# Fused adaLN, attention and Mish MLP: Mish stages moved between ScalarE and VectorE, and fixed probability buffers

## The chip, the cores and the metric

The kernel runs on one core of a Trainium2 chip. The metric is the device time of one execution in microseconds (us). The core has five engines with instruction queues of their own: TensorE (PE in the profile, with PEld for its weight loads), VectorE (DVE), ScalarE (ACT), GpSimd (POOL) and SyncE (SP), which here issues the DMAs. Each engine works its queue in order; engines wait for each other by semaphores. Three runs of the kernel before took 1747.57, 1747.98 and 1752.33 us; the median is 1747.98.

## The reference

One transformer block over a sequence of 2048 positions of width 512, in fp32. Shifts, scales and gates come from a conditioning vector.

```
mod = silu(c) @ w_mod                       # sa, ca, ga, sb, cb, gb
h = layernorm(x) * (1 + ca) + sa
q, k, v = split(h @ wqkv)                   # 32 heads of 16
p = softmax(q k^T / 4);  o = p v
x = x + ga * (o @ wo)
h = layernorm(x) * (1 + cb) + sb
t = h @ w1 + b1                             # 512 to 1792
act = t * tanh(softplus(t))                 # Mish
x = x + gb * (act @ w2)                     # 1792 to 512
```

## The kernel before

**Attention.** Queries are taken in four blocks of 512, heads in eight groups of four: 32 pairs of block and group (n), each in 16 steps over the keys, so 512 steps t (T), with 20 (PRO) ahead of them that only compute maxima, and a few behind. In a step (function `step`), TensorE computes four score products for the current pair (line 507; ScalarE takes their exponentials at line 510), four products for the maxima of scores 20 steps ahead (line 470; VectorE reduces each at line 472), and at the end of the step the values' product of the step two back (`pv`, line 525; four matmuls that the trace shows as eight). The scores contract over half of the array's rows, so the score and maximum products use one half, and beside them, on the other half, run matmuls of other work.

**Other work.** Everything else of the layer is cut into units: projections to q, k and v, the output projection (`wo_unit`), the up products of the MLP (`up_unit`, one for each of 14 tiles f of 128 features) and the down products (`down_unit`). A unit has 12 or 15 matmuls over the full 128 rows; `step` issues them as matmuls on 64 rows (`mm_half`, line 132), first half of the unit on the lower rows and then on the upper rows: six beside each step for four steps (a unit of 12), or eight and seven (a unit of 15). All accumulate in one PSUM bank, `bk`. When the last matmul of a unit is issued, its `fin` issues what empties the bank: for an up unit the ScalarE instruction of line 701 (`s1`), for the output projection the VectorE addition of line 770. The bank must be empty before the next unit begins. Steps with no unit ready run the eight products on both halves.

**Ring of banks.** Scores, maxima and single products go through a ring of six PSUM banks (`ring`); a product takes the bank of the sixth product before it, and so waits for the exponential or reduction that read it.

**What sets the order.** The program is written out in the order in which the generator calls the engines; a scheduler does not reorder it. Functions are hung on half-steps: `at(h, f)`, where h = 2t is the start of step t and h = 2t + 1 its middle, after the first half of the products. `done["a", f]` is the half-step at which the activation of tile f counts as ready; a down unit is queued five half-steps after that of its last tile. `cur["after"]` holds the instruction for which the first unit matmul of the next step waits: the consumer of the product issued beside the previous step's last unit matmul, where `product()` returns one. Scores return their exponential, maxima return nothing.

**Mish.** Function `mish` computes for a tile, with e = exp of the capped input: hb = t (line 701), the clamp (704, Relu of 10 - t on ScalarE), ee = exp(10 - clamp) (707), ee = ee (ee + 2) (710, VectorE), hb = hb ee (711, POOL), rr = ln(ee + 2) (714), rr = exp(-rr) (717), then on POOL one Newton step for the reciprocal and the product (723 to 727), and the split of the result into a high and a low part, `a_h` (95) and `a_l` (98). The stages after `s1` stand at half-steps 1, 2, 3, 4 and 6 behind it. In the last query block, behind the loop, the function `tail` runs the same on ScalarE and VectorE.

**MLP blocks in the loop.** The output projection, layernorm and MLP of query blocks 0 to 2 are units in the loop (3 x 14 = 42 up units); the fourth block and the end of the third are in `tail`: output projection (895), layernorm (104 to 109), the down units still held back (126, 829, 830), then the fourth MLP.

**Probability buffers.** Each exponential writes a tile `pr` from a pool, three in rotation for heads 0 and 2 of a group, four for 1 and 3. Reusing one waits for the values' product that read it.

Of the kernel before, what the change touches and what calls it, by code (L numbers as in the profile page):

```python
# [18 lines left out]
def adaln_block(ctx: ExitStack, tc: tile.TileContext, x, wqkv, wo, w1, b1, w2, c, w_mod, out):  # L19
# [442 lines left out]
    def max_tile(n, j, s, qs, kb):  # L462

        if n not in mxs:
            mxs[n] = ap.tile([P, 2, 8, 4], F32, tag="mx", name="mx", bufs=2)

        def product():
            kt, qt = ka[(2 * n + j) % NR], qa[(2 * n + j) % NR]
            pm = ring()
            nc.tensor.matmul(pm, qt[64 * s:64 * s + 64, qs * P:(qs + 1) * P], kt[64 * s:64 * s + 64, kb * TB:(kb + 1) * TB],  # L470
                             start=True, stop=True)
            nc.vector.tensor_reduce(out=mxs[n][:, s, 4 * j + qs, kb:kb + 1], in_=pm, op=ALU.max, axis=AX.X)  # L472

        return product

# [22 lines left out]
                        mt[o:o + 8, :].bitcast(F32))  # L498
        at(2 * (16 * n + 16 - PRO) + 3, put)

    pts = {}

    def score(n, j, s, kc):
        def product():
            kt, qt = ka[(2 * n + j) % NR], qa[(2 * n + j) % NR]
            p_ = ring()
            nc.tensor.matmul(p_, kt[64 * s:64 * s + 64, kc * P:(kc + 1) * P], qt[64 * s:64 * s + 64, :],  # L507
                             start=True, stop=True)
            pr = ap.tile([P, TB], F32, tag=f"p{2 * j + s}", name="pr", bufs=3 + s)
            e = nc.scalar.activation(pr, p_, AF.Exp, scale=SCALE)  # L510
            pts[16 * n + kc, 2 * j + s] = pr
            return e
        return product
# [173 lines left out]
    def mish(f, acc, tail):  # L687

        mp = mst["p"]
        hb = mp.tile([P, TB], F32, tag="hb", name="hb", bufs=3)  # L690
        ee = mp.tile([P, TB], F32, tag="ee", name="ee", bufs=2)
        rr = mp.tile([P, TB], F32, tag="rr", name="rr", bufs=2)
        qq = mp.tile([P, TB], F32, tag="qq", name="qq", bufs=1)
        a_h = mp.tile([P, TB], F32R, tag="a_h", name="a_h", bufs=NA)
        a_l = mp.tile([P, TB], F32R, tag="a_l", name="a_l", bufs=NA)

        def s1(late=False):
            if late:
                nc.vector.tensor_scalar_add(hb, acc, b1c[:, f:f + 1])
            else:  # L700
                nc.scalar.activation(hb, acc, AF.Identity, bias=b1c[:, f:f + 1])

        def s2():
            nc.scalar.activation(ee, hb, AF.Relu, bias=hcap, scale=-1.0)

        def s2b():
            nc.scalar.activation(ee, ee, AF.Exp, bias=hcap, scale=-1.0)  # L707

        def s3():
            nc.vector.scalar_tensor_tensor(ee, ee, 2.0, ee, op0=ALU.add, op1=ALU.mult)  # L710
            (nc.vector if tail else nc.gpsimd).tensor_mul(hb, hb, ee)  # L711

        def s4():
            nc.scalar.activation(rr, ee, AF.Ln, bias=two)

        def s5():
            nc.scalar.activation(rr, rr, AF.Exp, scale=-1.0)  # L717
            if tail:
                nc.vector.scalar_tensor_tensor(qq, ee, 2.0, rr, op0=ALU.add, op1=ALU.mult)
                nc.vector.scalar_tensor_tensor(rr, qq, 2.0, rr, op0=ALU.subtract, op1=ALU.mult)  # L720
                nc.vector.scalar_tensor_tensor(hb, hb, -1.0, rr, op0=ALU.mult, op1=ALU.mult)
            else:
                nc.gpsimd.tensor_scalar(ee, ee, 1.0, 2.0, op0=ALU.mult, op1=ALU.add)
                nc.gpsimd.tensor_mul(qq, ee, rr)  # L724
# [3 lines left out]
            hi_copy("v" if tail and f > FT - 4 else "p", a_h, hb)  # L728
            lo_sub("v" if tail and f > FT - 4 else "p", a_l, hb, a_h)

        return (a_h, a_l), (s1, s2, s2b, s3, s4, s5)

    def idle(h):

        return h is not None and 2 * (T - PRO) + 2 < h <= 2 * T
# [4 lines left out]
    def block(qb, t0):  # L740
# [61 lines left out]
        def up_unit(f, tag):  # L802
            w = w1s.pop(f)
            acc = bank(tag)
            up_mms(acc, w, *hx)
            act[f], stages = mish(f, acc, False)

            def fin(h):
                stages[0](idle(h))
                for i, s in zip((1, 2, 3, 4, 6), stages[1:]):  # L810
                    at(h + i, s)
                done["a", f] = h + 6
                if f == FT - 1 and qb == NB - 2:
# [62 lines left out]
    def tail():  # L876

        oh, ol = o_hl[last]
        mp = mst["p"]
        y, xn = [], []  # L880
        for v in (y, xn):
            for i in range(4):
                v.append(ap.tile([P, D], F32, tag=f"p{i}", name="y", bufs=3 + i % 2))
        for i in range(4):
            r = 4 * last + i
            nc.sync.dma_start(y[i], x[r * P:(r + 1) * P, :])
# [140 lines left out]
    def step(t):  # L1027
        second = t % 2
        n, u = t // 16, t % 16 // 2
        tm = t + PRO  # L1030
        run_hooks(2 * t)
        if t < 0:

            for i in range(2):
                if tm < 16:
                    kb, jq = divmod(2 * tm + i, 8)
                else:
                    jq, kb = tm % 16 // 2, 2 * second + i
# [24 lines left out]
        if tm < T:  # L1063
            o = max(0, (8 - f) // 2)
            mo, alone = maxima(tm // 16, tm % 16 // 2, s, o)

            mine = [x for p in zip(mo, own) for x in p] + own[len(mo):]
        else:
            o = max(0, (4 - f) // 2)
            mine = own[o:] if second else own[:4 - o]  # L1070
            alone = others[4 - o:] if second else others[:o]

            m = len(mine)
            if f > m:
# [131 lines left out]
    for pp, h in ((2, -22), (3, -8)):  # L1206
        at(h, lambda pp=pp: load_pair(pp))
    def run_hooks(h):
        for f in hooks.pop(h, []):
            f()  # L1210

    for t in range(-PRO, T + 2):
        step(t)
# [34 lines left out]
```

## Time and profile before

| | |
|---|---|
| median of three runs | 1747.98 us |
| the profiled execution, span | 1752.7 us |
| TensorE busy | 1711.7 us |
| VectorE busy | 1464.5 us |
| ScalarE busy | 1341.6 us |
| GpSimd busy | 751.4 us |
| attention exponentials (line 510) | 2048, mean 604 ns |
| reductions of maxima (line 472) | 2048, mean 683 ns |

The profiled execution is one further execution with the hardware profiler on; times of trace rows are microseconds from its start. A row of the timeline reads: start, duration, engine, line, operation, output<-inputs, shapes, count of equal instructions in a row, and in brackets how long the engine stood idle before and what released it. A matmul's row shows its modelled end, so successive rows overlap. The granted TensorE clock was full (0.996 on the mean).

### The profile page before, as it was taken

How to read it: one execution, taken by the hardware profiler on the slowest of the kernel's cores; microseconds unless marked ns; L12 is line 12 of the kernel's file. 1: busy time of each engine (PE TensorE's matmuls, PEld its weight loads, DVE VectorE, ACT ScalarE, POOL GpSimd, SP SyncE). 2: the span in 40 equal slices, each digit the busy share in tenths (PEclk: the TensorE clock that was granted, in tenths of full speed). 3: DMA queues.
4: the chain of work that ended last, by engine and by line, in shares of the span. 5: the costliest groups of instructions: out<-in, count | busy, mean ns of one | idle time of the engine just before them, and what ended most of it. 6: DMA issues, size and time to landing. Idle time of an engine off the chain costs nothing.

```text
span 1752.7 us, 33365 instructions
## 1 busy us (share of the span) xinstructions
PE 1711.7 (98%) x12230; PEld 954.7 (54%) x12230; DVE 1464.5 (84%) x2464; ACT 1341.6 (77%) x2565; POOL 751.4 (43%) x740
## 2 busy tenths in 40 slices
PE   7999999999999999999999999999999999999999
PEld 5755665555435455555455455555455455554687
DVE  6888888887888998888989898888989899891477
ACT  6247777777777898797877898797877799897464
POOL 5145224656303275263312276173412267162852
PEclk9999999999999999999999999999999999999999
DMA  7676467777662342432435443442435434422451
GB/s 236 181 234 196 119 170 208 236 238 220 207 196 63 110 117 71 143 101 67 104 108 144 126 114 80 121 120 52 120 82 158 113 102 102 126 79 71 153 228 61
DMA packets 113996, 240.05 MB, mean 137 GB/s; under 512 B 24048, under 2 KB 49648, under 8 KB 107784
## 3 DMA queue, kind: packets, MB, share of 16 engines
q1 hardware_dynamic: 113832, 237.92, 47.5%
q8 instruction: 96, 1.57, 0.4%
q14 instruction: 68, 0.56, 0.1%
HBM read 179.95 MB, written 51.44 MB: 132 GB/s over the span
## 4 chain that ended last, share of the span: by engine, by line
PE 80%; DMA 6%; DVE 4%; ACT 3%; POOL 3%; issue 2%; SPq 2%; POOLq 0%; ACTq 0%; DVEq 0%
PE bk L525 26%; PE ring L470 20%; PE ring L507 18%; PE bk L132 11%; DVE mx L472 3%; ACT pr L510 2%; DMA qscr<-ql 2%; PE ring L126 2%; PE ring L963 1%; PE bk L126 1%; DMA kscr<-ql 1%; DMA wr<-in_A_wqkv 1%; DMA w2scr<-hl 1%; DMA vg<-vscr 0%; SPq L317 0%
## 5 line engine op out<-in xcount | busy, mean ns | idle before, releaser
L472 DVE TENSOR_REDUCE mx<-ring 128x1 f32<-128x512 f32 x2048 | 1273.9, 683 | 176.9 <-PE ring L470 145.1
L510 ACT ACTIVATE pr<-ring 128x512 f32<-128x512 f32 x2048 | 1080.7, 604 | 274.7 <-PE bk L132 148.2
L470 PE MATMUL ring<-ka,qa 64*128 64x512 f32 x2048 | 847.6, 431 | 1.1 <-DVE mx L472 0.2
L507 PE MATMUL ring<-qa,ka 64*128 64x512 f32 x2048 | 737.4, 401 | 11.8 <-ACT pr L510 10.5
L470 PEld LDWEIGHTS ring<-ka,qa 64*128 64x128 f32 x2048 | 364.8, 184 | 398.3 <-DVE mx L472 321.8
L525 PE MATMUL bk<-pr,vg 128*32 128x512 f32 x4096 | 547.0, 606 | 0.0
L507 PEld LDWEIGHTS ring<-qa,ka 64*128 64x128 f32 x2048 | 372.5, 185 | 119.9 <-ACT pr L510 64.3
L132 PE MATMUL bk<-h,w 64*128 64x512 f32 x996 | 275.9, 409 | 1.4 <-ACT pr L510 1.2
L132 PEld LDWEIGHTS bk<-h,w 64*128 64x128 f32 x996 | 171.1, 184 | 17.5 <-ACT pr L510 7.7
L132 PE MATMUL bk<-w,a_h 64*128 64x512 f32 x576 | 167.2, 414 | 0.3
L525 PEld LDWEIGHTS bk<-pr,vg 128*32 128x32 f32 x4096 | 80.7, 108 | 138.6 <-issue 133.4
L830 POOL TENSOR_TENSOR y<-yd,y 128x512 f32<-128x512 f32 x40 | 51.9, 1303 | 214.2 <-ACT yd L829 193.6
L711 POOL TENSOR_TENSOR hb<-hb,ee 128x512 f32<-128x512 f32 x42 | 53.9, 1284 | 178.2 <-DVE ee L710 178.2
L132 PEld LDWEIGHTS bk<-w,a_h 64*128 64x128 f32 x576 | 96.4, 184 | 12.0 <-ACT pr L510 6.7
L724 POOL TENSOR_TENSOR qq<-ee,rr 128x512 f32<-128x512 f32 x42 | 54.4, 1295 | 75.3 <-ACT rr L717 72.7
L132 PE MATMUL bk<-w,o_hl 64*128 64x512 f32 x288 | 80.6, 411 | 1.6 <-POOL o_hl L95 1.0
L132 PE MATMUL bk<-w,a_l 64*128 64x512 f32 x288 | 76.9, 390 | 0.0
L98 POOL TENSOR_TENSOR a_l<-hb,a_h 128x512 fp32r<-128x512 f32 x53 | 72.3, 1363 | 4.4
L132 PE MATMUL bk<-h_h,wl 64*128 64x512 f32 x168 | 57.2, 421 | 0.0
L710 DVE SCALAR_TENSOR_TENSOR ee<-ee 128x512 f32<-128x512 f32 x56 | 39.8, 711 | 19.3 <-ACT ee L707 19.3
L727 POOL TENSOR_TENSOR hb<-hb,rr 128x512 f32<-128x512 f32 x42 | 54.4, 1296 | 3.3
L132 PEld LDWEIGHTS bk<-w,a_l 64*128 64x128 f32 x288 | 53.0, 184 | 4.8
(186 smaller groups left out, 1735.8 us busy)
## 6 DMA issues: line engine op xcount, KB each, us to landing
ka<-kscr SPq DMA_DIRECT2D x124, 384.0 KB
w<-w2scr SPq DMA_DIRECT2D x56, 512.0 KB
w<-w1scr SPq DMA_DIRECT2D x46, 512.0 KB
vg<-vscr SPq DMA_DIRECT2D x32, 552.0 KB
qa<-qscr SPq DMA_DIRECT2D x124, 100.0 KB
kscr<-qh SPq DMA_DIRECT2D x16, 512.0 KB
qscr<-qh SPq DMA_DIRECT2D x32, 256.0 KB
hl<-in_B_w SPq DMA_DIRECT2D x28, 256.0 KB
```

What stands on the lines that cost most here:

```text
L98: (nc.gpsimd if eng == "p" else nc.vector).tensor_sub(lo, src, hi.bitcast(F32))
L126: nc.tensor.matmul(acc, l, r, start=start, stop=stop)
L132: i = nc.tensor.matmul(acc, l[64 * g:64 * g + 64], r[64 * g:64 * g + 64], start=start, stop=stop)
L470: nc.tensor.matmul(pm, qt[64 * s:64 * s + 64, qs * P:(qs + 1) * P], kt[64 * s:64 * s + 64, kb * TB:(kb + 1) * TB], start=True, stop=True)
L472: nc.vector.tensor_reduce(out=mxs[n][:, s, 4 * j + qs, kb:kb + 1], in_=pm, op=ALU.max, axis=AX.X)
L507: nc.tensor.matmul(p_, kt[64 * s:64 * s + 64, kc * P:(kc + 1) * P], qt[64 * s:64 * s + 64, :], start=True, stop=True)
L510: e = nc.scalar.activation(pr, p_, AF.Exp, scale=SCALE)
L525: nc.tensor.matmul(accs[n][32 * h:32 * h + 32, :], vgs[n][:, o:o + 32], pts.pop((t, h)), start=(kc == 0), stop=(kc == 15))
L711: (nc.vector if tail else nc.gpsimd).tensor_mul(hb, hb, ee)
L724: nc.gpsimd.tensor_mul(qq, ee, rr)
L727: nc.gpsimd.tensor_mul(hb, hb, rr)
L830: nc.gpsimd.tensor_add(y[i], yd, y[i])
```

## The change

1. In `mish`, outside of `tail`: the clamp becomes a VectorE instruction, min(t, 10); the exponential then has no bias; the product on VectorE is made in two halves of 256 columns, with POOL's product behind the second. The stages after `s1` (clamp, exponential, first half, second half, logarithm, reciprocal) stand at half-steps 0, 1, 2, 4, 5 and 11 behind it; late in the loop at 0, 1, 2, 3, 4 and 6. `done["a", f]` follows the last of these. Tiles are taken from their pools where they are first written.
2. `fin` is called before the last product beside a unit is issued, not after. If the last two products of the other half beside the unit are a maximum and a score, they change places. A maximum now returns its reduction, so it can be the instruction that the next step's first unit matmul waits for.
3. The probability tiles are fixed buffers by head and step, the same number as before, and the dependency of an exponential on the exponential that wrote its buffer before is declared unnecessary, as the values' product in between is waited for. `tail` uses the same buffers for its rows.
4. Half-step functions hung on the half-step that is running are run too (`run_hooks`).

```diff
-            nc.vector.tensor_reduce(out=mxs[n][:, s, 4 * j + qs, kb:kb + 1], in_=pm, op=ALU.max, axis=AX.X)
+            return nc.vector.tensor_reduce(out=mxs[n][:, s, 4 * j + qs, kb:kb + 1], in_=pm, op=ALU.max, axis=AX.X)
...
-            pr = ap.tile([P, TB], F32, tag=f"p{2 * j + s}", name="pr", bufs=3 + s)
+            h, b = 2 * j + s, (16 * n + kc) % (3 + s)
+            if h not in prs:
+                prs[h] = [ap.tile([P, TB], F32, name=f"pr{h}_{i}") for i in range(3 + s)]
+            pr = prs[h][b]
             e = nc.scalar.activation(pr, p_, AF.Exp, scale=SCALE)
+            if (h, b) in exps:
+                tc.declare_no_dep(e.ins, exps[h, b].ins, reason="the values' product between them reads it")
+            exps[h, b] = e
...
         def s2():
-            nc.scalar.activation(ee, hb, AF.Relu, bias=hcap, scale=-1.0)
+            ee = buf("ee", 2)
+            if tail:
+                nc.scalar.activation(ee, b["hb"], AF.Relu, bias=hcap, scale=-1.0)
+            else:
+                nc.vector.tensor_scalar(ee, b["hb"], HCAP, 0.0, op0=ALU.min, op1=ALU.add)
 
         def s2b():
-            nc.scalar.activation(ee, ee, AF.Exp, bias=hcap, scale=-1.0)
-
-        def s3():
-            nc.vector.scalar_tensor_tensor(ee, ee, 2.0, ee, op0=ALU.add, op1=ALU.mult)
-            (nc.vector if tail else nc.gpsimd).tensor_mul(hb, hb, ee)
+            if tail:
+                nc.scalar.activation(b["ee"], b["ee"], AF.Exp, bias=hcap, scale=-1.0)
+            else:
+                nc.scalar.activation(b["ee"], b["ee"], AF.Exp)
+
+        def s3(v=None):
+            c = slice(0, TB) if v is None else slice(v * TB // 2, (v + 1) * TB // 2)
+            e = b["ee"][:, c]
+            nc.vector.scalar_tensor_tensor(e, e, 2.0, e, op0=ALU.add, op1=ALU.mult)
+            if v != 0:
+                (nc.vector if tail else nc.gpsimd).tensor_mul(b["hb"], b["hb"], b["ee"])
...
             def fin(h):
-                stages[0](idle(h))
-                for i, s in zip((1, 2, 3, 4, 6), stages[1:]):
+                s1, s2, s2b, s3, s4, s5 = stages
+                s1(idle(h))
+                when = (0, 1, 2, 3, 4, 6) if h > 2 * (T - PRO) + 2 else (0, 1, 2, 4, 5, 11)
+                for i, s in zip(when, (s2, s2b, lambda: s3(0), lambda: s3(1), s4, s5)):
                     at(h + i, s)
-                done["a", f] = h + 6
+                done["a", f] = h + when[-1]
...
             mine = [x for p in zip(mo, own) for x in p] + own[len(mo):]
+            kinds = [k for p in zip("m" * len(mo), "s" * len(mo)) for k in p] + ["s"] * (len(own) - len(mo))
+            if 2 <= f <= len(mine) and kinds[f - 1] == "s" and kinds[f - 2] == "m":
+                mine[f - 2:f] = mine[f - 1], mine[f - 2]
...
         def emit(product):
             e = product()
-            if e is not None and cur.pop("want", None):
+            if cur.pop("want", None):
                 cur["after"] = e
...
                 if last:
+                    if second and not cur["left"]:
+                        cur["fin"](2 * t + 2)
+                        cur["fin"] = None
                     cur["want"] = True
                     if i < len(mine):
                         emit(mine[i])
-                    if second and not cur["left"]:
-                        cur["fin"](2 * t + 2)
-                        cur["fin"] = None
```

In the program's order ScalarE has, around one up unit in the loop of the kernel before (line 701 empties the bank, 704 is the clamp, 707 the exponential, 714 the logarithm, 717 the reciprocal):

```order
L701 ACTIVATE hb<-bk,b1c 128x512
L510 ACTIVATE pr<-ring 128x512 x2
L704 ACTIVATE ee<-hb,hcap 128x512
L510 ACTIVATE pr<-ring 128x512 x3
L707 ACTIVATE ee<-ee,hcap 128x512
L510 ACTIVATE pr<-ring 128x512 x4
L714 ACTIVATE rr<-ee,two 128x512
L510 ACTIVATE pr<-ring 128x512 x4
L717 ACTIVATE rr<-rr 128x512
```

and at such a place of the changed kernel (707 empties the bank, 720 is the exponential, 735 the reciprocal of the unit before, 730 the logarithm; `pr_2_1177` and the like are the fixed buffers):

```order
L707 ACTIVATE hb<-bk,b1c 128x512
L513 ACTIVATE pr_0_1182<-ring 128x512
L513 ACTIVATE pr_2_1151<-ring 128x512
L720 ACTIVATE ee<-ee 128x512
L513 ACTIVATE pr_2_1159<-ring 128x512
L513 ACTIVATE pr_3_1152<-ring 128x512
L513 ACTIVATE pr_3_1160<-ring 128x512
L513 ACTIVATE pr_1_1176<-ring 128x512
L735 ACTIVATE rr<-rr 128x512
L513 ACTIVATE pr_1_1183<-ring 128x512
```

The exponential stands where the clamp stood, the place of the old exponential is empty, and the reciprocal has moved to the middle of a later step, in the next unit. On VectorE the kernel before has, in the steps of the first up units, the reductions and the whole product:

```order
L472 TENSOR_REDUCE mx<-ring 128x1 x26
L710 SCALAR_TENSOR_TENSOR ee<-ee 128x512
L472 TENSOR_REDUCE mx<-ring 128x1 x14
L560 RECIPROCAL rc<-sm 128x16
L472 TENSOR_REDUCE mx<-ring 128x1 x2
L710 SCALAR_TENSOR_TENSOR ee<-ee 128x512
```

and the changed kernel the clamp (714) and the two halves of the product (725), each at the start of a step:

```order
L472 TENSOR_REDUCE mx<-ring 128x1 x20
L714 TENSOR_SCALAR ee<-hb 128x512
L472 TENSOR_REDUCE mx<-ring 128x1 x4
L725 SCALAR_TENSOR_TENSOR ee<-ee 128x256
L472 TENSOR_REDUCE mx<-ring 128x1 x4
L725 SCALAR_TENSOR_TENSOR ee<-ee 128x256
L472 TENSOR_REDUCE mx<-ring 128x1 x8
L714 TENSOR_SCALAR ee<-hb 128x512
```

Three VectorE instructions stand in three successive steps where one stood in the middle of a step. At the end of the loop TensorE has in the kernel before (126 are a unit's matmuls over all rows, here the end of tile 13's; 895 is the output projection of `tail`):

```order
L525 MATMUL bk<-pr,vg 32x512 x8
L126 MATMUL bk<-h_15991,w_19305 128x512 x2
L126 MATMUL bk<-h_15992,w_19305 128x512 x4
L525 MATMUL bk<-pr,vg 32x512 x4
L895 MATMUL bk<-ka_635,o_hl 128x512 x2
```

and in the changed kernel (531 is the values' product, `w_16906` the weights of tile 12, `w_17378` of tile 13, 912 the output projection):

```order
L126 MATMUL bk<-h_14485,w_16906 128x512 x2
L126 MATMUL bk<-h_14486,w_16906 128x512 x4
L126 MATMUL bk<-h_14485,w_17378 128x512 x2
L531 MATMUL bk<-pr_1_1176,vg 32x512
L531 MATMUL bk<-pr_3_1152,vg 32x512
L531 MATMUL bk<-pr_1_1183,vg 32x512
L531 MATMUL bk<-pr_3_1160,vg 32x512
L126 MATMUL bk<-h_14485,w_17378 128x512 x6
L126 MATMUL bk<-h_14486,w_17378 128x512 x4
L912 MATMUL bk<-ka_635,o_hl 128x512 x2
```

The up unit of tile 13, which in the kernel before ends within the loop's last steps, is now almost whole behind the last step with scores, and tile 12's end has its place.

More of the change, by code (lines that the diff above doesn't have):

```diff
@@ L689, in mish, with buf @@
         mp = mst["p"]
[L690 to L695, printed above, removed]
+        b, a = {}, []
+        def buf(tag, bufs, dt=F32):
+            if tag not in b:
+                b[tag] = mp.tile([P, TB], dt, tag=tag, name=tag, bufs=bufs)
+            return b[tag]
@@ L697, in s1 @@
         def s1(late=False):
             if late:
-                nc.vector.tensor_scalar_add(hb, acc, b1c[:, f:f + 1])
+                nc.vector.tensor_scalar_add(buf("hb", 3), acc, b1c[:, f:f + 1])
             else:
-                nc.scalar.activation(hb, acc, AF.Identity, bias=b1c[:, f:f + 1])
+                nc.scalar.activation(buf("hb", 3), acc, AF.Identity, bias=b1c[:, f:f + 1])
         def s2():
-            nc.scalar.activation(ee, hb, AF.Relu, bias=hcap, scale=-1.0)
-        def s2b():
-            nc.scalar.activation(ee, ee, AF.Exp, bias=hcap, scale=-1.0)
@@ L713, in s4 @@
+        def s3(v=None):
[4 more added lines that the diff above has]
+                (nc.vector if tail else nc.gpsimd).tensor_mul(b["hb"], b["hb"], b["ee"])
         def s4():
-            nc.scalar.activation(rr, ee, AF.Ln, bias=two)
+            nc.scalar.activation(buf("rr", 2), b["ee"], AF.Ln, bias=two)
         def s5():
+            hb, ee, rr, qq = b["hb"], b["ee"], b["rr"], buf("qq", 1)
+            a.extend(mp.tile([P, TB], F32R, tag=tag, name=tag, bufs=NA) for tag in ("a_h", "a_l"))
@@ L727, in s5 @@
                 nc.gpsimd.tensor_mul(hb, hb, rr)
-            hi_copy("v" if tail and f > FT - 4 else "p", a_h, hb)
-            lo_sub("v" if tail and f > FT - 4 else "p", a_l, hb, a_h)
-        return (a_h, a_l), (s1, s2, s2b, s3, s4, s5)
+            hi_copy("v" if tail and f > FT - 4 else "p", a[0], hb)
+            lo_sub("v" if tail and f > FT - 4 else "p", a[1], hb, a[0])
+        return a, (s1, s2, s2b, s3, s4, s5)
     def idle(h):
@@ L879, in tail @@
         mp = mst["p"]
[L880 to L883, printed above, removed]
+        y, xn = ([prs[i][(T + v) % (3 + i % 2)] for i in range(4)] for v in range(2))
         for i in range(4):
@@ L1208, in run_hooks @@
     def run_hooks(h):
-        for f in hooks.pop(h, []):
-            f()
+        while h in hooks:
+            for f in hooks.pop(h):
+                f()
     for t in range(-PRO, T + 2):
```

2 lines of the change are left out of this document (1 added, 1 removed).

## The prediction

> **What bounds the kernel now.** I read the page first: the busy line and the chain that ended last.
>
> ```profile
> span 1752.7 us, 33365 instructions
> ...
> PE 1711.7 (98%) x12230; PEld 954.7 (54%) x12230; DVE 1464.5 (84%) x2464; ACT 1341.6 (77%) x2565; POOL 751.4 (43%) x740
> ...
> PE 80%; DMA 6%; DVE 4%; ACT 3%; POOL 3%; issue 2%; SPq 2%; POOLq 0%; ACTq 0%; DVEq 0%
> PE bk L525 26%; PE ring L470 20%; PE ring L507 18%; PE bk L132 11%; DVE mx L472 3%; ACT pr L510 2%; DMA qscr<-ql 2%; PE ring L126 2%; PE ring L963 1%; PE bk L126 1%; DMA kscr<-ql 1%; DMA wr<-in_A_wqkv 1%; DMA w2scr<-hl 1%; DMA vg<-vscr 0%; SPq L317 0%
> ```
>
> The chain lies on TensorE for 80%: values' product (L525), maxima (L470), scores (L507), unit matmuls (L132). An edit on another engine therefore counts only where a step of the loop is longer than its matmuls. The timeline, cut at the values' products, shows how long a step is. First two neighbours without MLP work, and the first and the last of 77 like the longer one:
>
> ```profile
> 122.66 1.07 PE L525 MATMUL bk<-pr,vg 128*32 128x512 f32 x8
> ...
> 314.00 1.06 PE L525 MATMUL bk<-pr,vg 128*32 128x512 f32 x8
> ...
> 315.33 0.39 PE L507 MATMUL ring<-qa,ka 64*128 64x512 f32 x1
> ...
> 315.82 2.06 ACT L510 ACTIVATE pr<-ring 128x512 f32<-128x512 f32 x4 [0.83 <-PE bk L132]
> ...
> 316.89 1.07 PE L525 MATMUL bk<-pr,vg 128*32 128x512 f32 x8
> ...
> 318.22 0.39 PE L507 MATMUL ring<-qa,ka 64*128 64x512 f32 x1
> ...
> 318.65 2.06 ACT L510 ACTIVATE pr<-ring 128x512 f32<-128x512 f32 x4 [0.26 <-PE bk L132]
> ...
> 319.72 1.07 PE L525 MATMUL bk<-pr,vg 128*32 128x512 f32 x8
> ...
> 1523.27 1.06 PE L525 MATMUL bk<-pr,vg 128*32 128x512 f32 x8
> ```
>
> One step takes 2.89, the next 2.83. In the first the exponentials begin 0.10 after the end of their score (315.72 to 315.82), in the second 0.04 (318.61 to 318.65). The listing of the line's instructions has semaphore waits of their own ahead of about a quarter of the exponentials:
>
> ```profile
> L510 ACTq EVENT_SEMAPHORE  x553: 17/17/1687, 111.4 to 1616.7; - x185
> ```
>
> Then four steps' start around an up unit of the MLP, by the same timeline:
>
> ```profile
> 1129.26 1.06 PE L525 MATMUL bk<-pr,vg 128*32 128x512 f32 x8
> ...
> 1129.65 0.69 ACT L701 ACTIVATE hb<-bk,b1c 128x512 f32<-128x512 f32 x1
> ...
> 1130.39 0.49 PE L132 MATMUL bk<-h,w 64*128 64x512 f32 x1
> ...
> 1130.79 2.48 DVE L472 TENSOR_REDUCE mx<-ring 128x1 f32<-128x512 f32 x4 [0.41 <-PE ring L470]
> ...
> 1131.51 0.71 ACT L704 ACTIVATE ee<-hb,hcap 128x512 f32<-128x512 f32 x1
> ...
> 1132.21 1.07 PE L525 MATMUL bk<-pr,vg 128*32 128x512 f32 x8
> ...
> 1133.56 0.74 ACT L707 ACTIVATE ee<-ee,hcap 128x512 f32<-128x512 f32 x1
> ...
> 1134.17 2.07 ACT L510 ACTIVATE pr<-ring 128x512 f32<-128x512 f32 x4
> ...
> 1135.27 1.07 PE L525 MATMUL bk<-pr,vg 128*32 128x512 f32 x8
> ```
>
> The step from 1129.26 takes 2.95, the one from 1132.21 takes 3.06. The excess over 2.84 is the bound to work on: 0.11, because the bank that L701 empties is free only at 1130.34 and the next unit's first matmul comes at 1130.39; and 0.22, because the clamp (L704) and the MLP exponential (L707) push the four attention exponentials to 1134.17 (a maximum later in the step takes the bank which the first of them empties).
>
> **The change, part by part.** *One activation per step.* The clamp leaves ScalarE and the MLP exponential moves into the clamp's old place, behind the first attention exponential of the step from 1129.26. The start of the next step is then free: 0.22 gone. 39 units have this pattern (42 with the in-loop form, three of them late in the loop, where the old spacing stays): 39 x 0.22 = 8.6 gained. Ends: 0, if another wait takes its place, and 10.
>
> *Fixed probability buffers.* The exponentials lose the second wait, and 2.89 becomes 2.83: 77 x 0.055 = 4.2 gained. About 30 of these steps lie ahead of 460 us, where the chain also shows DMA waits (qscr, kscr) that could swallow part: ends 2.4 and 4.5.
>
> *Bank emptied sooner.* In the order ScalarE still has three exponentials, then the emptying of the bank, then the fourth. The 0.11 stays; I count nothing. For the output projection the emptying is VectorE's addition, and it does come one reduction earlier:
>
> ```profile
> 556.41 0.68 DVE L770 TENSOR_TENSOR y<-bk,y 128x512 f32<-128x512 f32 x1
> ...
> 556.96 0.18 PEld L470 LDWEIGHTS ring<-ka,qa 64*128 64x128 f32 x1 [0.84 <-DVE mx L472]
> ...
> 557.14 0.18 PEld L132 LDWEIGHTS bk<-w,o_hl 64*128 64x128 f32 x1
> ...
> 559.61 3.65 DVE L472 TENSOR_REDUCE mx<-ring 128x1 f32<-128x512 f32 x6
> ...
> 559.97 0.50 PE L132 MATMUL bk<-w,o_hl 64*128 64x512 f32 x1
> ```
>
> The unit's matmul at 557.14 follows the addition's end (557.09), while the maximum beside it began at 556.96. With the addition one reduction (0.6) earlier, 0.16 of the 0.18 goes, in 9 units (the fourth of each block has no such follower): 1.4 gained.
>
> *The dependency that is paid for it.* The first unit matmul of a step waits for whoever consumes the product beside the previous step's last unit matmul: an exponential before, now the third maximum's reduction (fourth where seven or eight unit matmuls run). At 559.61 that is the first reduction of the six, since the layernorm statistics sit ahead of it; it ends at 559.61 + 0.68 = 560.29, and with the 0.05 of 1130.34 to 1130.39 the matmul of 559.97 could begin at 560.34. So 0.37 lost, in 9 steps: 3.4. Ends: 0 and 5. For the steps with eight unit matmuls:
>
> ```profile
> 1094.68 2.48 DVE L472 TENSOR_REDUCE mx<-ring 128x1 f32<-128x512 f32 x4 [0.56 <-PE ring L470]
> ...
> 1097.21 0.49 PE L132 MATMUL bk<-w,a_h 64*128 64x512 f32 x1
> ```
>
> The fourth reduction ends at 1097.16, 0.05 ahead of the matmul that will wait for it: no room at all. I take 0.02 for each of 64 such steps, 1.3 lost; ends 0 and 3. In plain steps there is room: the third reduction of those from 1130.79 ends near 1132.65 (three quarters of 2.48), the next step's matmuls begin about 1.0 behind 1132.21, at 1133.2.
>
> *Clamp and halves on VectorE.* The old product and a POOL instruction that it met, then the MLP chain on POOL:
>
> ```profile
> L710 DVE SCALAR_TENSOR_TENSOR ee<-ee x56: 668/683/1595, 603.4 to 1740.6; 128x512 f32<-128x512 f32 x56
> ...
> 638.50 1.29 POOL L568 TENSOR_TENSOR od<-od,rb 128x512 f32<-128x512 f32 x1
> ...
> 639.05 1.28 DVE L710 SCALAR_TENSOR_TENSOR ee<-ee 128x512 f32<-128x512 f32 x1
> ...
> 1139.75 1.29 POOL L724 TENSOR_TENSOR qq<-ee,rr 128x512 f32<-128x512 f32 x1 [2.05 <-ACT rr L717]
> ...
> 1145.29 1.30 POOL L98 TENSOR_TENSOR a_l<-hb,a_h 128x512 fp32r<-128x512 f32 x1
> ```
>
> A full instruction takes 0.68 free, a half about 0.35 (an estimate from it), the clamp at most 0.68. VectorE idles 0.41 in a step (1130.79), and its third reduction has the 0.5 of room above: hidden as long as nothing else holds it. At 639.05 something did: the product ended 0.54 after L568's end (639.79), so it stood 0.6 behind POOL. The Trainium skill, "SBUF — State Buffer", section "Who interferes with whom", says that VectorE and GpSimd share a port pair as an exclusive lock held for the whole instruction, and that a tensor_scalar or a VectorE instruction with two SBUF inputs takes it. The wait of 0.6 agrees; by that rule the clamp may wait too, which the old clamp on ScalarE could not. How long, hangs on the spacing. POOL's chain takes 6.84 (1139.75 to 1146.59) from the reciprocal's end. That activation now stands behind the first attention exponential of the step from 1132.21, one unit later: exponential near 1133.95 to 1134.5, activation to 1135.1, chain 1135.25 to 1142.1. The next unit's clamp has its place in the step that begins at 1129.26 + 2.95 + 3 x 2.84 = 1140.7; the reductions ahead of it end 1.1 later (1133.27 against 1132.21), as does the bank's emptying, so it asks near 1141.85. POOL's last instruction then holds it for 0.2 to 0.3, which the 0.5 covers. Where a transposition of maxima lengthens a step the places slip: six units x 0.3 = 1.8 lost, ends 0 and the rival below.
>
> *The end of the loop.* The down units wait five half-steps longer, so two steps without unit work are added twice, and the last up unit's twelve matmuls fall behind the loop. There POOL works off one chain after another:
>
> ```profile
> 1622.16 1.28 POOL L711 TENSOR_TENSOR hb<-hb,ee 128x512 f32<-128x512 f32 x1 [13.98 <-DVE ee L710]
> ...
> 1634.47 1.28 POOL L711 TENSOR_TENSOR hb<-hb,ee 128x512 f32<-128x512 f32 x1
> ...
> 1643.67 1.29 POOL L711 TENSOR_TENSOR hb<-hb,ee 128x512 f32<-128x512 f32 x1
> ...
> 1651.75 1.29 POOL L98 TENSOR_TENSOR a_l<-hb,a_h 128x512 fp32r<-128x512 f32 x1
> ...
> 1668.12 1.67 PE L126 MATMUL ring<-w,a_h 128*128 128x512 f32 x6 [0.30 <-ACT yd L829]
> ```
>
> A chain takes 9.2 (1634.47 to 1643.67). The last ends at 1653.04, the final layernorm's small POOL instructions queue behind it, and TensorE, otherwise dense, waits for the result at 1668.12. With all of the last block four steps (11.3) later, the first chain reaches POOL near 1633.5 instead of 1622.16, and the place at 1634.47 which the second had is its: everything behind is one chain later less 1.0, that is 8.2 lost. Ends: 3 (twelve more matmuls in TensorE's stream alone, by the six in 1.67 of the last row) and 9.5 (a whole chain and some of its waits).
>
> **The sum.** Gained 8.6 + 4.2 + 1.4 = 14.2. Lost 8.2 + 3.4 + 1.3 + 1.8 = 14.7. Net 0.5 more. The profiled execution took 1752.7, 4.7 above the median of the runs shown (1747.98), near the highest of them; the terms are differences inside it, so I add them to the median: 1748.5. The bound below which this kernel's measurement hardly tells a change is 0.3%, 5.2 us.
>
> **Rivals.** *The tail hides it.* If POOL's chain has slack I do not see, the tail costs the 3 of the matmuls, and the net is 0.5 - 5.2 = -4.7: 1743. Against it stands the wait at 1668.12; for it, that the wait is only 0.30. If the VectorE dependency also costs nothing (a consumer that always ends in time), 4.7 more go: 1738.
>
> *POOL's lock takes the clamp in every unit.* It decides once POOL's last instruction of a chain ends before the clamp asks: then the next, ready product of 1.29 starts first, the clamp waits for all of it, the third reduction ends 1.3 - 0.5 = 0.8 after the matmul that waits for it. 39 x 0.8 = 31: 1779. Against it: the 0.2 to 0.3 worked out above lie on the good side; for it, that the margin is that small. By the skill's rule the lock makes this possible at all.
>
> *The second step keeps its excess.* If the moved exponential still delays what follows, 8.6 fall away: 1757. Against it: a step has 0.8 idle on ScalarE (315.82), and the instruction 0.74.
>
> **How the numbers follow.** My sum, within 0.3%: 0.45. Tail or dependency hidden, 1738 to 1743: 0.30, of which 0.27 is faster by over 0.3%. Excess kept, part of the lock, or more dependency than counted, 1753 to 1760: 0.18; the lock in full: 0.07. Faster 0.29, same 0.46, slower 0.25. The range of eight in ten reaches from 1738 to 1758; the likeliest case alone is 1744 to 1753.
>
> **What would show it.** After: exponentials without waits of their own and no 2.89 steps; the step after an up unit's first near 2.84, with the first still 2.95; matmuls of the output projection released by VectorE; clamp durations mostly under 0.7 with a few near 1.3; and the last product's chain on POOL ending some 8 after what the loop gives. Clamps of 1.3 or more throughout, or steps of 3.5 in the MLP, would make the forecast wrong upwards; a TensorE that runs densely through the tail would make it wrong downwards.

## The result and the profile after

The changed kernel takes 1750.13 us (median of 12 runs, 1748.48 to 1753.29) against 1748.3 for the kernel before in the same comparison: a ratio of 1.0013, 95% interval 1.0003 to 1.0022, so about 2.3 us slower (0.5 to 3.8). Nothing was gained, though a good deal moved. The page of the changed kernel, the lines that answer to those of before:

```profile
span 1748.4 us, 32922 instructions
...
PE 1701.2 (97%) x12218; PEld 942.5 (54%) x12218; DVE 1498.4 (86%) x2548; ACT 1312.6 (75%) x2523; POOL 754.9 (43%) x740
...
PE 81%; DVE 8%; DMA 5%; ACT 3%; POOL 2%; issue 1%; SPq 0%; POOLq 0%; DVEq 0%; ACTq 0%
PE bk L531 26%; PE ring L470 19%; PE ring L507 18%; PE bk L132 10%; DVE mx L472 5%; PE bk L126 3%; PE ring L126 2%; DMA qscr<-ql 2%; ACT pr L513 2%; PE ring L980 1%; DMA w2scr<-hl 1%; DMA hl<-in_B_w 1%; DMA wma<-in_w_mod 0%; DVE ee L714 0%; DMA vg<-vscr 0%
```

VectorE's share of the chain doubles, from 4% to 8%: DVE mx, that is the reductions, and a little DVE ee L714, the clamp. Around an up unit the timeline now has:

```profile
1125.97 1.07 PE L531 MATMUL bk<-pr,vg 128*32 128x512 f32 x8
1126.34 0.70 ACT L707 ACTIVATE hb<-bk,b1c 128x512 f32<-128x512 f32 x1
...
1127.15 0.43 DVE L714 TENSOR_SCALAR ee<-hb 128x512 f32<-128x512 f32 x1
...
1128.26 0.62 ACT L720 ACTIVATE ee<-ee 128x512 f32<-128x512 f32 x1
...
1128.91 1.07 PE L531 MATMUL bk<-pr,vg 128*32 128x512 f32 x8
...
1131.74 1.07 PE L531 MATMUL bk<-pr,vg 128*32 128x512 f32 x8
```

The first step is still 2.94, the second 2.83 where it was 3.06. Added over the 39 units, the second steps' excess over the length of their matmuls (2.84 with six unit matmuls, 3.04 with eight, 2.74 with none) falls from 9.9 to 0.7. Four of these steps also held a transposition of maxima before and none does after; a step with one and six unit matmuls takes 3.05 or more in both kernels. Without these four the excess falls from 9.0 to 0.7, so 8.3 is gained. That gain is given back at two places. One is the clamp, in six of its steps; one of them, and then a step in which it goes well:

```profile
1052.85 1.29 POOL L98 TENSOR_TENSOR a_l<-hb,a_h 128x512 fp32r<-128x512 f32 x1
1053.08 1.07 PE L531 MATMUL bk<-pr,vg 128*32 128x512 f32 x8
...
1054.10 1.29 POOL L727 TENSOR_TENSOR hb<-hb,ee 128x512 f32<-128x512 f32 x1
1054.31 1.36 DVE L714 TENSOR_SCALAR ee<-hb 128x512 f32<-128x512 f32 x1
...
1056.76 1.06 PE L531 MATMUL bk<-pr,vg 128*32 128x512 f32 x8
```

```profile
1029.73 1.07 PE L531 MATMUL bk<-pr,vg 128*32 128x512 f32 x8
1029.74 1.29 POOL L98 TENSOR_TENSOR a_l<-hb,a_h 128x512 fp32r<-128x512 f32 x1
...
1030.89 0.43 DVE L714 TENSOR_SCALAR ee<-hb 128x512 f32<-128x512 f32 x1
1030.98 1.50 POOL L727 TENSOR_TENSOR hb<-hb,ee 128x512 f32<-128x512 f32 x1
```

In the first, POOL's chain ended 0.17 ahead of the clamp (1054.14 against 1054.31), POOL's next product began, the clamp took 1.36 and its step 3.68. In the second the chain ended behind the clamp's turn (1031.03), the clamp took 0.43, and the step 2.94. The other place is the end. From the last pair of values' products on, first before, then after:

```profile
1633.56 1.92 PE L525 MATMUL bk<-pr,vg 128*32 128x512 f32 x16
```

```profile
1620.73 1.92 PE L531 MATMUL bk<-pr,vg 128*32 128x512 f32 x16
...
1639.40 1.74 POOL L727 TENSOR_TENSOR hb<-hb,ee 128x512 f32<-128x512 f32 x1
...
1647.46 1.29 POOL L98 TENSOR_TENSOR a_l<-hb,a_h 128x512 fp32r<-128x512 f32 x1
...
1650.91 0.50 PE L126 MATMUL ring<-w,a_l 128*128 128x512 f32 x1 [1.30 <-DVE pr L925]
...
1652.88 0.96 PE L126 MATMUL ring<-w,a_h 128*128 128x512 f32 x3 [0.79 <-DVE pr L925]
...
1663.83 1.66 PE L126 MATMUL ring<-w,a_h 128*128 128x512 f32 x6 [1.31 <-ACT yd L849]
```

From there to the end it was 1752.7 - 1633.56 = 119.1, and is 1748.4 - 1620.73 = 127.7: 8.5 more. From the first values' product to there it was 1517.1 and is 1508.1: 9.0 less. The changed kernel's profiled execution also began its loop 3.9 sooner, which is not put down to the change: over the profiles of this study the first values' product begins anywhere from 111.2 to 116.5 us. So the two profiled executions differ by 4.3 one way and the medians by 2.3 the other; single executions of the kernel before lie up to 8 apart (1744.27 to 1752.33), and only the medians are compared as times.

### The profile page after: what moved, and what is told of

Same layout as the page of the kernel before. It is cut to its first block, busy times and chain, and to the rows that moved or that the text cites. A ratio compares the mean times of both kernels' runs of the same rounds, so it can differ in the third digit from the quotient of the medians.

```text
span 1748.4 us, 32922 instructions
## 1 busy us (share of the span) xinstructions
PE 1701.2 (97%) x12218; PEld 942.5 (54%) x12218; DVE 1498.4 (86%) x2548; ACT 1312.6 (75%) x2523; POOL 754.9 (43%) x740
## 4 chain that ended last, share of the span: by engine, by line
PE 81%; DVE 8%; DMA 5%; ACT 3%; POOL 2%; issue 1%; SPq 0%; POOLq 0%; DVEq 0%; ACTq 0%
PE bk L531 26%; PE ring L470 19%; PE ring L507 18%; PE bk L132 10%; DVE mx L472 5%; PE bk L126 3%; PE ring L126 2%; DMA qscr<-ql 2%; ACT pr L513 2%; PE ring L980 1%; DMA w2scr<-hl 1%; DMA hl<-in_B_w 1%; DMA wma<-in_w_mod 0%; DVE ee L714 0%; DMA vg<-vscr 0%
## 5 line engine op out<-in xcount | busy, mean ns | idle before, releaser
L470 PE MATMUL ring<-ka,qa 64*128 64x512 f32 x2048 | 793.9, 428 | 0.9
L132 PE MATMUL bk<-h,w 64*128 64x512 f32 x972 | 268.8, 409 | 0.5 <-ACT pr L513 0.5
L132 PEld LDWEIGHTS bk<-h,w 64*128 64x128 f32 x972 | 167.2, 184 | 12.8 <-ACT pr L513 4.2
L727 POOL TENSOR_TENSOR hb<-hb,ee 128x512 f32<-128x512 f32 x42 | 58.2, 1385 | 157.4 <-DVE ee L725 157.4
L725 DVE SCALAR_TENSOR_TENSOR ee<-ee 128x256 f32<-128x256 f32 (+1 forms) x98 | 53.9, 553 | 8.1 <-ACT ee L718 4.8
L744 POOL TENSOR_TENSOR rr<-rr,qq 128x512 f32<-128x512 f32 x42 | 54.1, 1287 | 3.5
```

The costliest lines, as they stand in the source:

```text
L132: i = nc.tensor.matmul(acc, l[64 * g:64 * g + 64], r[64 * g:64 * g + 64], start=start, stop=stop)
L725: nc.vector.scalar_tensor_tensor(e, e, 2.0, e, op0=ALU.add, op1=ALU.mult)
L727: (nc.vector if tail else nc.gpsimd).tensor_mul(b["hb"], b["hb"], b["ee"])
```

## The experiments

All are edits of the changed kernel unless said otherwise. Ratios are to the kernel before; the changed kernel's is 1.0013, and 0.001 is 1.75 us.

**Fixed buffers alone**, on the kernel before (the third part of the change and nothing else).

> The kernel before with the fixed probability buffers alone. If the second wait of the exponentials costs 0.055 in each of 77 steps, it comes out 4.2 below the kernel before, near 1744, and no step without MLP work lies at 2.89. If DMA waits of the first 460 us take back what is gained there, 2.4 are left: 1746. If the wait only shows in the trace and something else sets those steps, no difference.

1744.55, ratio 0.9975 (0.9965 to 0.9986): 4.4 less. The exponentials' own waits are gone, and none of the 77 steps is left at 2.89:

```profile
L513 ACTq EVENT_SEMAPHORE  x6: 17/17/38, 106.1 to 1576.9; - x6
```

So this part alone is worth 4.4, and it is faster than the whole change.

**Tile 13 spaced as before.**

```diff
-when = (0, 1, 2, 3, 4, 6) if h > 2 * (T - PRO) + 2 else (0, 1, 2, 4, 5, 11)
+when = (0, 1, 2, 3, 4, 6) if h > 2 * (T - PRO) + 2 or f == FT - 1 else (0, 1, 2, 4, 5, 11)
```

> The changed kernel, but the last up unit of each MLP block (tile 13) keeps the old half-steps 0, 1, 2, 3, 4 and 6, so the steps without unit work are not added and tile 13 of the third block ends in the loop again. If the loop's end costs what the chain of POOL instructions is late (8.2 us in the prediction), this comes out about 8 below the changed kernel, near 1742. If only the matmuls behind the loop count, it gains 3 and comes out near 1747. If the end of the loop is hidden, no difference from 1750.

1748.77, ratio 0.9995 (0.9984 to 1.0007): 3 below the changed kernel by the ratios, though their intervals overlap, and near the value of the second case. Yet the trace shows the first: the end takes 118.6 again, all of the 8.5 and a little more. The loop is longer by 6.5, of which 5.3 lie in the down units' first steps and most of the rest in the steps of the clamps, of which seven are long (1.03 to 1.53). What the unit matmuls (line 132) stood idle for lists a releaser that neither the kernel before nor the changed one has:

```profile
  POOL a_h L95: 6.7, 4
```

Tile 12's chain on POOL, still spaced late, now runs just ahead of tile 13's, and the down units come before their operand. So the steps added in the change gave POOL the time that it needs in the inner blocks.

**Without the second part** (maxima return nothing, products in the old order, bank emptied behind the last product).

> The changed kernel without its second part: maxima return nothing, the last two products keep their places, and the bank is emptied behind the last product, so the first unit matmul of a step waits for an exponential again. By the terms of the prediction it regains 3.4 in the output projection's steps and 1.3 in the steps of eight and seven unit matmuls and loses the 1.4 of the earlier addition: 3.3 below the changed kernel, near 1747. If the dependency costs nothing, it is 1.4 slower than the changed kernel, near 1751.5.

1760.36, ratio 1.0076 (1.0055 to 1.0097): 11 slower than the changed kernel, where both cases had said within 3.3. The run takes out the three edits of this part together, so it does not say what each is worth. The clamps tell where the time goes, in the listing of their line (shortest, median, longest in ns), the changed kernel first:

```profile
L714 DVE TENSOR_SCALAR ee<-hb x42: 404/429/1369, 591.2 to 1630.1; 128x512 f32<-128x512 f32 x42
```

```profile
L714 DVE TENSOR_SCALAR ee<-hb x42: 404/428/1580, 589.9 to 1640.1; 128x512 f32<-128x512 f32 x42
```

Sixteen of them take 0.91 to 1.58, where six do in the changed kernel (1.02 to 1.37). One of the ten new ones:

```profile
1030.79 1.28 POOL L98 TENSOR_TENSOR a_l<-hb,a_h 128x512 fp32r<-128x512 f32 x1
1030.88 1.07 PE L531 MATMUL bk<-pr,vg 128*32 128x512 f32 x8
...
1032.03 1.30 POOL L727 TENSOR_TENSOR hb<-hb,ee 128x512 f32<-128x512 f32 x1
1032.07 1.54 DVE L714 TENSOR_SCALAR ee<-hb 128x512 f32<-128x512 f32 x1
```

POOL's product begins 0.04 ahead of the clamp and holds it for all of its length. What moved the clamp back against POOL is seen in the step ahead, which now waits for an exponential; here such a one of the same run:

```profile
1138.25 0.71 ACT L730 ACTIVATE rr<-ee,two 128x512 f32<-128x512 f32 x1
...
1138.86 1.56 ACT L513 ACTIVATE pr<-ring 128x512 f32<-128x512 f32 x3
...
1139.82 0.18 PEld L470 LDWEIGHTS ring<-ka,qa 64*128 64x128 f32 x1 [0.84 <-DVE mx L472]
...
1139.99 0.50 PE L132 MATMUL bk<-h,w 64*128 64x512 f32 x1
```

The logarithm stands ahead of three of the four exponentials. The second of the three (the step's third) ends near 1139.9, and the unit's first matmul comes 0.17 behind the maximum that could begin at 1139.82. With the reduction as releaser both begin together, as in the changed kernel:

```profile
1135.58 0.49 PE L470 MATMUL ring<-ka,qa 64*128 64x512 f32 x1
...
1135.58 0.50 PE L132 MATMUL bk<-h,w 64*128 64x512 f32 x1
```

In the ten new cases the step ahead of the clamp takes 2.91 to 2.97, where such a step takes 2.84 in the changed kernel. The clamp asks about a tenth later, and POOL's chain is over by then.

**Reciprocal half a step sooner** (half-step 10 in place of 11).

> The changed kernel with the reciprocal at half-step 10 in place of 11, so POOL's chain begins about 0.7 to 1.2 us sooner and its last instruction should end before the next unit's clamp asks for VectorE's turn. If POOL and VectorE exclude each other there, the next POOL product starts first, most clamps take about 1.3 in place of 0.43, the step of the clamp grows by some 0.7, and the kernel is about 27 us slower (39 units), near 1777. If there is no such lock, clamps stay at 0.43 and the time stays near 1750.

1756.51 in a single run, 7.3 above the kernel before: slower, but not by 27. The clamps do not meet the beginning of POOL's product but its end, and a half of the product on VectorE meets another POOL instruction instead:

```profile
1148.43 1.30 POOL L744 TENSOR_TENSOR rr<-rr,qq 128x512 f32<-128x512 f32 x1
1148.60 1.41 DVE L725 SCALAR_TENSOR_TENSOR ee<-ee 128x256 f32<-128x256 f32 x1
...
1166.07 1.28 POOL L727 TENSOR_TENSOR hb<-hb,ee 128x512 f32<-128x512 f32 x1
...
1166.90 0.73 DVE L714 TENSOR_SCALAR ee<-hb 128x512 f32<-128x512 f32 x1
```

The exclusion is there, its place was misjudged: I had put POOL's product at the clamp's turn, and it ends by then.

**POOL's product held, first try** (the same product, issued with the reciprocal), and the same on the kernel without the second part, in all units.

> The changed kernel, but in one unit of four (the one whose following unit's clamp stands behind a step lengthened by the transposition of maxima) POOL's product t ee waits until the reciprocal, so POOL has nothing to run when that clamp asks. If POOL holds VectorE off there, the five clamps of 1.13 to 1.37 next to that step fall to 0.43, their steps shorten by 0.5 to 0.75 each, and the kernel gains 3.5 over the changed one: 1746.5. If the long clamps have another cause, they stay and so does the time, 1750.

> The changed kernel without its second part (which took 1760 against 1750), with POOL's product held until the reciprocal in all units of the loop. If the 10 us are clamps of 1.36 to 1.58 that start behind POOL's product in ten more units, they go with the product out of the way, and it comes out near 1750 to 1752. If the 10 us are the exponentials' dependency itself, it stays near 1760.

1751.11 (ratio 1.0013) and 1762.98 (1.0078): no difference either time. The edit changed nothing on POOL, where this product is the next instruction in any case and waits for nothing else.

**POOL's product held behind a wait.** In units whose next clamp follows a lengthened step, POOL first multiplies with the reciprocal, which it must wait for:

```diff
-            if v != 0:
+            if v != 0 and not b["held"]:
...
+            elif b["held"]:
+                nc.gpsimd.tensor_mul(hb, hb, rr)
+                nc.gpsimd.tensor_mul(hb, hb, ee)
+                nc.gpsimd.tensor_scalar(ee, ee, 1.0, 2.0, op0=ALU.mult, op1=ALU.add)
+                nc.gpsimd.tensor_mul(qq, ee, rr)
+                nc.gpsimd.tensor_scalar(qq, qq, -1.0, 2.0, op0=ALU.mult, op1=ALU.add)
+                nc.gpsimd.tensor_mul(hb, hb, qq)
...
+                s1(idle(h), h <= 2 * (T - PRO) + 2 and h // 2 % 16 == 10)
```

> The changed kernel, with POOL's product of one unit in four moved behind the first product with the reciprocal, so that it now stands behind a wait and cannot run when the next clamp asks (the earlier try left POOL's order as it was, since the product was the next instruction there anyway). If POOL holds VectorE off, the clamps of 1.13 to 1.37 in the steps from 723, 1053, 1149 and 1433 us and their like fall under 0.6, and the kernel gains 3.5 over the changed one: 1746.5. If not, clamps and time stay.

1747.32, ratio 0.9994 (0.9981 to 1.0007): 3.3 below the changed kernel. The intervals overlap a little, but the trace agrees: six long clamps become two, and the first steps' excess falls from 8.2 to 5.7.

```profile
L715 DVE TENSOR_SCALAR ee<-hb x42: 403/427/1372, 589.7 to 1625.8; 128x512 f32<-128x512 f32 x42
```

The two left (1.37 at 624.64, 1.25 at 992.80) begin behind POOL instructions of the attention (line 574, ending at 625.73, and line 98, ending at 993.76), and end 0.28 and 0.29 after them. So it need not be the Mish product that holds the clamp.

**The same in all units, without the second part.**

> The changed kernel without its second part, with POOL's product held behind the reciprocal's wait in all units of the loop. Without the hold that kernel took 1760, with 16 clamps of 0.91 to 1.58. If these clamps are its loss, ten or more of them fall under 0.8 and it comes out near 1751 to 1753; if the exponentials' dependency is, it stays at 1760.

1751.86, ratio 1.0011 (0.9999 to 1.0022), against 1.0076 without the hold: 11 back.

```profile
L715 DVE TENSOR_SCALAR ee<-hb x42: 403/427/874, 594.3 to 1635.0; 128x512 f32<-128x512 f32 x42
```

Sixteen clamps of 0.91 to 1.58 became four of 0.83 to 0.87, with POOL doing the same number of instructions. That POOL's product holds the clamp off is shown by this pair. What the second part is worth apart from it is the rest, some 3 by the ratios (1.0011 against 0.9994 with the part and with the hold in one unit of four; the intervals overlap): in the trace without it the fourth step of a unit has 0.13 of excess, 5.5 in the sum over units against 2.5.

**Tiles 12 and 13 of the third block on VectorE**, then both edits together with the first form of the hold, then tile 12 alone.

```diff
-            act[f], stages = mish(f, acc, False)
+            act[f], stages = mish(f, acc, qb == NB - 2 and f > FT - 3)
```

> The changed kernel, but tiles 12 and 13 of the third block (the last two up units, at the end of the loop and behind it) run their product, Newton step and split on VectorE, which has no maxima left there, in place of POOL. If the 8 us that the end of the changed kernel is longer are POOL's chain of instructions, the chain is gone, TensorE is dense there but for the 3 us of the added matmuls and the waits for the bank, and the kernel comes out 5 below the changed one, near 1745. If TensorE's own stream sets the end, no difference: 1750.

> Both edits on the changed kernel: VectorE in place of POOL for the last two tiles, and POOL's product held back in one unit of four. If the two act in different places the gains add, 5 + 3.5: near 1741.5, below the kernel before (1748) by 0.35%. If the loop's gain is taken back at the end or the other way, 1745 to 1747.

> The changed kernel, with tile 12 of the third block alone on VectorE for product, Newton step and split; tile 13 stays on POOL. The run with both on VectorE lost 3 us because the final output projection's operands, split on VectorE, queued behind tile 13's instructions there (TensorE idle 5.25 at 1642). With tile 12 alone VectorE is free by then, and POOL has two chains in place of three: its last should end 8 to 9 sooner, no wait for the layernorm is left, and the end of the kernel takes 3 (the added matmuls and the wait for the bank) more than in the kernel before, not 8.5: 1745. If TensorE's stream sets the end all the same, 1750.

Both tiles: 1754.23 (1.0020, 1.0011 to 1.0030), no faster than the changed kernel, with an end of 131.0 in place of 127.7; and with the edit that did nothing 1753.84 (1.0030, 1.0018 to 1.0041). Tile 12 alone: 1747.82 (1.0000, 0.9987 to 1.0012), 2.3 below the changed kernel by the ratios, with intervals that overlap; its end takes 124.7 in place of 127.7. TensorE's waits, with both and with tile 12 alone:

```profile
1647.22 2.90 PE L912 MATMUL bk<-ka,o_hl 128*128 128x512 f32 x6 [5.25 <-issue]
```

```profile
1630.77 2.36 PE L912 MATMUL bk<-ka,o_hl 128*128 128x512 f32 x9 [0.78 <-ACT hb L707]
...
1642.94 1.16 PE L912 MATMUL bk<-ka,o_hl 128*128 128x512 f32 x4 [1.01 <-DVE o_hl L98]
```

With both, the split of the last heads' result stood behind tile 13's instructions on VectorE, and TensorE waited 5.25 for it (VectorE's timeline has tile 13's last instruction end at 1642.48; a reciprocal and a product follow, and the split's first instruction ends at 1647.12). With one, the waits for the layernorm (1650.91, 1652.88) and the one at 1663.83 are gone; 5.5 are left of the 8.5: the twelve matmuls, twice 0.78 for the bank and 1.01 for the split. So POOL's chain is 3 of the 8.5 when the rest of the added work stays, and all 8.5 go when that goes too.

**A faster version.** Beside the hold (with a second place for units that stand at other steps), the down units are ready five half-steps sooner, and their matmuls go tile by tile, so that the last tile is needed by the last three only:

```diff
-            mm3(acc, [act[f][0][:, s] for f in fs], [act[f][1][:, s] for f in fs],
-                [w2s[f][:, 0, :] for f in fs], [w2s[f][:, 1, :] for f in fs])
+            seq = [m for f in fs for m in ((act[f][0], 0), (act[f][0], 1), (act[f][1], 0))]
+            for j, (l, v) in enumerate(seq):
+                mm(acc, l[:, s], w2s[fs[j // 3]][:, v, :], j == 0, j == len(seq) - 1)
...
-                queue(lambda l=fs[-1]: done.get(("a", l), 4 * T) + 5, lambda tag, gi=gi, i=i: down_unit(gi, i, tag))
+                queue(lambda l=fs[-1]: done.get(("a", l), 4 * T), lambda tag, gi=gi, i=i: down_unit(gi, i, tag))
...
-                s1(idle(h))
+                s1(idle(h), h <= 2 * (T - PRO) + 2 and h // 2 % 16 in (8, 10))
```

> The changed kernel with POOL's product held in the units whose clamp follows a lengthened step (steps 8 and 10 of 16, as the held run, one more place for the other alignment), and with the down units ready five half-steps sooner, their matmuls put in order by tile so that the last tile, the one that POOL finishes last, is needed only by their last three matmuls. The order then has tile 13 of the third block in the loop again, with none of the four added steps. If the 8.5 us at the end came from these steps alone and TensorE meets no wait for POOL's a_l, this gains 8.5 and 3.3 over the changed kernel: 1738, 0.6% below the kernel before. If TensorE waits for POOL in the two inner blocks as with tile 13 respaced (some 2.6 each), 1743 to 1745. If the end is not regained, 1747.

1740.70, ratio 0.9956 (0.9942 to 0.9970): 7.7 below the kernel before and 10 below the changed one. The end takes 118.6 and no matmul waits for `a_h`:

```profile
1622.62 1.92 PE L531 MATMUL bk<-pr,vg 128*32 128x512 f32 x16
...
1640.04 1.29 POOL L98 TENSOR_TENSOR a_l<-hb,a_h 128x512 fp32r<-128x512 f32 x1
```

Between the last pair of values' products and the end of the last chain there are now 18.7 (1641.33 - 1622.62), where the changed kernel has 28.0. The time is 2.7 above the first case. In the trace the second steps of the units have some 2 more of excess than with the hold alone, as halves of the product meet POOL there (the step from 1019.81 takes 3.51). Against the fixed buffers alone (ratio 0.9975) the gain is 3.3, with intervals that overlap by 0.0005: of the 7.7, more than half is what the third part of the change brings by itself.

## Why the prediction was right, and where it was not

The forecast was 0.5 more than before, in a range of 1738 to 1758; measured are 2.3 more. The terms, one by one:

- Second step of an up unit, -8.6: right. 9.0 of excess became 0.7, a gain of 8.3.
- Fixed buffers, -4.2: right, 4.4 when made alone.
- Bank emptied sooner for up units, 0: right, the first steps stay at 2.94.
- Output projection, -1.4 and +3.4 (9 x 0.37 is 3.3): right in sum. The three steps ahead of a transposition of the layernormed rows took 2.89 + 3.00 + 2.98 and take 2.84 + 2.85 + 3.40, 0.22 more, or 2.0 for nine. Five of the nine groups are like it; of the others three also hold a transposition of maxima, and they do not compare one to one.
- Steps of eight and seven unit matmuls, +1.3: wrong, but small. Their excess was 2.8; it is 1.8, with four steps that a half of the product lengthened (1.1 together) set aside. But in both kernels four of the steps with eight are second steps of up units, which fell by 1.2 together and are in the first term already, and one with a long clamp, counted with the lock, adds some 0.6 to the 1.8. Without them the excess is the same within 0.4, and I count 0: the reduction releases the next step in time.
- End of the loop, +8.2: right in size, 8.5. The prediction's step took it for POOL's chain alone; the runs split it. POOL's chain is the last of three bounds there, and without it 5.5 remain, not 3, since two waits for the bank (0.78 each) and one for VectorE come forth.
- Lock between POOL and the clamp, +1.8: too small, and the term that was mis-sized. "Six units x 0.3" had the count right, six clamps, five of them behind a lengthened step as foreseen. But each costs 0.33 to 0.76, together 3.8, as POOL's next product runs whole ahead of the clamp; and halves of the product met POOL in seven places besides, some 2.5 together. One of these:

```profile
1071.94 1.28 POOL L742 TENSOR_TENSOR qq<-ee,rr 128x512 f32<-128x512 f32 x1 [3.16 <-ACT rr L735]
...
1072.36 1.15 DVE L725 SCALAR_TENSOR_TENSOR ee<-ee 128x256 f32<-128x256 f32 x1
```

With the sizes of the trace in place, the sum is -8.3 - 4.4 + 2.0 + 0 + 8.5 + 5.7 = 3.5, inside the interval of 0.5 to 3.8 (5.7 is the lock without the 0.65 that the second steps' 0.7 holds already). The lock came out 3.9 above its term, and the others together 0.9 below theirs. So the forecast was near because gains of some 13 were met by losses that it had priced, the end above all. That the lock's excess did not carry the time out of the likeliest case is luck: with 16 clamps caught, as without the second part, it would have. The sum is not closed in the trace: its terms in the loop make 5.0 less, and the loops of the two profiled executions differ by 9.0. What the other 4.0 are is not shown.

The rival in which the lock takes every clamp was closer than its 0.07 said: a delay of a tenth or two in the step ahead, and 16 of 39 are caught. What the prediction did not see is that the second part of the change is what keeps clamp and product apart. It costed that part by itself, as a loss of 3.3, and undoing it cost 11. By the rule of "SBUF — State Buffer" in the Trainium skill, section "Who interferes with whom", the one that comes first holds the ports for the whole instruction. The rows agree: the clamps of 1054.31 and 1032.07 both end 0.28 behind the end of the product that began ahead of them (1055.39 and 1033.33).

## What to carry to other kernels

Two engines that exclude each other made this schedule sensitive to a tenth of a microsecond. The cure was to put a wait in front of the instruction that must not run just then (1747.32); issuing it later in the program, with nothing new to wait for, moved nothing (1751.11). When a stage is spaced out to hide its latency, look what its last member now delays, at the end of the loop above all, and let the consumer take the late operand last. Make each part of a combined change alone as well: here one part gained 4.4 by itself, and the others lost more than that together.

## What the runs showed that I had not expected

The clamp took 0.43 on VectorE (median 429 ns) where the product over the same 128x512 takes 0.68, so it was cheaper than I had bounded it; a half of the product took about 0.42, more than the 0.35 estimated. And POOL suffers too: its product took 1.50 (1030.98) where it began behind a clamp, and 1.29 where it began ahead.
